# A gated linear recurrence followed by a two-layer MLP: 16-token rows of v read from the input, weight pieces laid out one by one, new due times

## The chip, the cores and the metric

The kernel runs on one core of a Trainium2 chip. The metric is device time in microseconds of one execution. The three runs of the kernel before took 986.98, 987.89 and 995.43 us; their median is 987.89 us.

## The reference

```python
mag = np.sqrt(a_re * a_re + a_im * a_im)
scale = np.minimum(mag, 0.999) / (mag + 1e-06)
a_re_n, a_im_n = (a_re * scale, a_im * scale)
...
for t in range(S):
    new_re = ar * S_re - ai * S_im
    new_im = ar * S_im + ai * S_re
    kv = np.einsum('bhd,bhe->bhde', k[:, :, t], v[:, :, t])
    S_re, S_im = (new_re + kv, new_im)
    y[:, :, t] = np.einsum('bhd,bhde->bhe', q[:, :, t], S_re)
...
x = np.ascontiguousarray(attn_out.transpose(0, 2, 1, 3)).reshape(B * S, H * D)
h = x @ w_in
g = np.maximum(h, 0.0) + alpha * np.minimum(h, 0.0)
return (g @ w_out).astype(np.float32)
```

There are 4 batches, 8 heads, 768 tokens and a head dimension of 48. x has 3072 rows of 384, w_in is 384 x 2048 and w_out 2048 x 384. The two weight matrices arrive as 64-bit floats; everything else is float32.

## The kernel before

**Units.** The 3072 tokens are cut into 24 units of 128 (4 batches x 6 chunks). A unit computes attention inside its chunk by levels: for h = 1, 2, 4, 8, 16, 32 the second half of each block of 2h tokens looks at the first half, and a state `St` carries what lies before the chunk. Six generators make one pipeline, and each engine executes in order what they gave it:

- `gates(b, c0, c1)`, nine in all: it normalizes the gates of one to three chunks, makes products of magnitudes (`decays_sb`, written to DRAM as `decs`) and running products of phases (written to DRAM as `phs`). Most of it is on ScalarE and VectorE; the products over short rows (L358, L360 with `blk`, `run`) are on GpSimd in all but the first gate.
- `loads()` (L614 to L632) brings q and k of a unit into `KQ` (three buffers), `phs` into `PP` (one buffer) and `decs` into `T` (two buffers).
- `half_rows()` (L598) copies v in DRAM into `vsc`, with only the first halves of blocks of h tokens, for each h in `SPREAD`; `loads_v()` (L641 to L664) brings v into `V`, and into `VL` the first halves for each level: for h = 1, 2, 32 straight from v (L661), for the h in `SPREAD` from `vsc` (L664). `V` and `VL` have two buffers.
- `pieces()` (L510) and `weights(name)` (L523 to L551) bring the weights in 8 pieces each of w_in and w_out, and turn 64-bit floats into float32: VectorE works on the bits (L528 to L541), PE adds high and low parts (L548, L549), ScalarE stores (L551).
- `unit(u)` (L681 to L850): the rotation of q and k by `PP` on VectorE (L681), the levels (PE L731 and L691; VectorE L735 to L750 and L711; ScalarE L708 and L756), keys transposed (L771, L775), the state (L783 to L799), the outputs `ps_y` (L823, L830), copied by ScalarE (L845) and written to DRAM as `ysc` (L850).
- `loads_x()` (L863) reads `ysc` back as `xT` for a group of units: groups of 1, 1, ten of 2, 1 and 1 units. `all_mlp()` gives each group 16 blocks of features (PE L874, ScalarE L882, VectorE L884), and the output matmuls L894, ScalarE L902, and L905 to DRAM.

**Order.** Nothing orders the work but the class `Plan`: every generator yields, ahead of each instruction, which engine it is for, what it costs and what it needs. The planner takes, of the steps that could start soonest, the one with the earliest due time. The due times are the numbers in `GATES_DUE`, `UNIT_DUE`, `UNIT_STEPS` and the two ends given to `plan.add`. All DMAs are issued by SyncE (SP), one after the other, in the planner's order; a DMA that has to wait for a buffer or for data holds up all that stand behind it.

Of the kernel before, what the change touches and what calls it, by code (L numbers as in the profile page):

```python
# [8 lines left out]
F32 = mybir.dt.float32  # L9
U32 = mybir.dt.uint32  # L10
AF = mybir.ActivationFunctionType
# [4 lines left out]
P = 128  # L16
# [115 lines left out]
def kernel(  # L132
# [32 lines left out]
    nc = tc.nc  # L165
    B, HP, _, D, S = q.shape
# [3 lines left out]
    NK = DM // P  # L170
# [54 lines left out]
    def DVE(n, *after, takes=(), first=False):  # L225
        return "DVE", 0.17 + n * 1.05e-3, after, takes, 0, first

    def ACT(n, *after, takes=(), first=False):
        return "ACT", 0.17 + n * 0.85e-3, after, takes, 0, first
# [29 lines left out]
    def gates(b, c0, c1):  # L259
# [66 lines left out]
        STT(out=dec[:, :, 0:P], in0=c.rearrange("p (m s) -> p m s", s=P), scalar=-2.0 * MAG_CAP,  # L326
            in1=f.rearrange("p (m s) -> p m s", s=P), op0=ALU.max, op1=ALU.mult)

        for o, (p, w) in enumerate(((y, -1.0), (x, 1.0), (y, 1.0))):
            tu = yield ACT(2.3 * N, tx, t)  # L330
            nc.scalar.activation(U3[:, o], p.rearrange("p (n l) -> p l n", l=L), AF.Copy, scale=w)  # L331
        at = 0
        while at < TL - 4:
            m = (TL - at) // 2
# [116 lines left out]
        done["gates", b + last, 0 if last else c1] = used  # L451


    w_in_sb = consts.tile([P, NK, DF], F32, tag="w_in_sb")
    w_out_sb = consts.tile([P, NF, DM], F32, tag="w_out_sb")


# [55 lines left out]
    def to_f32(dst, parts, scales, *key):  # L513

        n = 2 * DM
        ta = yield ACT(n, ("raw", *key), takes=(R["top"],))
        raw = raws.pop(key)
        lo, hi = raw[:, :, :, 0], raw[:, :, :, 1]
        rest = lo.bitcast(F32)
        slot = R["top"].taken  # L520
        top = tops[slot].rearrange("p (r e) -> p r e", r=dst.shape[1])
        top_u, dst_u = top.bitcast(U32), dst.bitcast(U32)
        nc.scalar.activation(top, hi.bitcast(F32), AF.Abs)  # L523
        tl = yield ACT(n, ta)
        nc.scalar.activation(rest, lo, AF.Copy, scale=2.0 ** -52)

        yield DVE(n // 2, ta)
        nc.vector.tensor_scalar(out=top, in0=top, scalar1=F64_SMALL, scalar2=None, op0=ALU.max)  # L528

        yield DVE(n * 3 // 4)  # L530
        nc.vector.tensor_scalar(out=dst_u, in0=top_u, scalar1=3, scalar2=0x3FFFFFFF,
                                op0=ALU.logical_shift_left, op1=ALU.bitwise_and)
        yield DVE(n)
        nc.vector.scalar_tensor_tensor(out=dst_u, in0=hi, scalar=0xC0000000, in1=dst_u,  # L534
                                       op0=ALU.bitwise_and, op1=ALU.bitwise_or)

        yield DVE(n * 3 // 4)
        nc.vector.tensor_scalar(out=top_u, in0=dst_u, scalar1=0xFF800000, scalar2=None,
                                op0=ALU.bitwise_and)
        t = yield DVE(n, tl)  # L540
        nc.vector.tensor_tensor(out=rest, in0=rest, in1=top, op=ALU.mult)  # L541
        R["top"].put(t, slot)
        for i, r in enumerate(parts):
            m, low = dst[:, r], rest[:, r]
            k = m.free_size()
            e = yield PE(k * 3.36e-3, t, takes=(R["h"],), n=2)
            p = ps.tile([P, 512], F32, tag="h", name="ps_w", bufs=2)[:, 0:k].rearrange("p (r e) -> p r e", r=m.shape[1])
            nc.tensor.matmul(p, lhsT=ident, rhs=m, start=True, stop=False)  # L548
            nc.tensor.matmul(p, lhsT=ident, rhs=low, start=False, stop=True)  # L549
            t_ = yield ACT(k, e)  # L550
            nc.scalar.activation(m, p, AF.Copy, scale=scales[i])  # L551
            R["h"].put(t_)
        raw_done(*key, e)
        return t_
# [11 lines left out]
    def weights(name):  # L566
        for f in range(NF // 2):
            if name == "in":
                dst, parts, scales = w_in_sb[:, :, 2 * f * P:2 * (f + 1) * P], (slice(0, 2), slice(2, 3)), (1.0, 1.0)
            else:  # L570
                dst, parts = w_out_sb[:, 2 * f:2 * (f + 1)], (slice(0, 1), slice(1, 2))
                scales = al_s[:, 2 * f:2 * f + 1], al_s[:, 2 * f + 1:2 * f + 2]
            done["w_" + name, 2 * f] = done["w_" + name, 2 * f + 1] = yield from piece(dst, parts, scales, name, f)


    KINDS = ["odd"] + LEVELS
    SPREAD = [4, 8, 16]
    vsc_of = {}

    def half_rows():  # L580
# [54 lines left out]
    def loads_v():  # L635
        for u in range(NU):
            b, c = divmod(u, NCH)
            yield DMA(196, ("KQ", u), takes=(R["V"],))
            L = loaded[u]
            L["V"] = V = work.tile([P, HP, D2], F32, tag="V", name="V", bufs=2)  # L640
            nc.sync.dma_start(V, v[b, :, :, c].rearrange("n p e -> p n e"))  # L641
            yield DMA(98)
            VL = work.tile([P, len(KINDS), 2, D2], F32, tag="VL", name="VL", bufs=2)
            first = True
            for k, h in enumerate(KINDS):
                for i in range(2):
                    tokens = v[b, 2 * i:2 * i + 2, :, c].rearrange("n t e -> t n e")
                    to = VL[HC * i:HC * (i + 1), k]
                    if h in ("odd", 1):
                        runs = [(to, tokens[int(h == "odd")::2])]  # L650
                    elif h == 2:
                        runs = [(to[j::2], tokens[j::4]) for j in range(2)]
                    elif h == 32:
                        runs = [(to[h * m:h * (m + 1)], tokens[2 * h * m:2 * h * m + h]) for m in range(2)]
                    else:
                        runs = []
                    for dst, src in runs:
                        if not first:
                            yield DMA(98 // len(runs))
                        first = False  # L660
                        nc.sync.dma_start(dst, src)  # L661
            t = yield DMA(98 * len(SPREAD), ("halves", u))
            k = KINDS.index(SPREAD[0])
            nc.sync.dma_start(VL[:, k:k + len(SPREAD)].rearrange("p l n e -> p l (n e)"),  # L664
                              vsc_of.pop(u).rearrange("l i t e -> (i t) l e"))
            L["Vp"] = {name: VL[:, i] for i, name in enumerate(KINDS)}
            done["V", u] = t
# [198 lines left out]
    def features(m, f):  # L866

        n = sizes[m] * P
        for kk in range(NK):
            e = yield PE(n * 1.68e-3, ("x", m), ("w_in", f), takes=() if kk else (R["h"],))  # L870
            if kk == 0:
                p = ps.tile([P, MT], F32, tag="h", name="ps_h", bufs=2)[:, 0:n]
            plan.pace = 1.0
            nc.tensor.matmul(p, lhsT=w_in_sb[:, kk, f * P:(f + 1) * P], rhs=x_of[m][:, kk],  # L874
                             start=(kk == 0), stop=(kk == NK - 1))
        if f == NF - 1:
            R["xT"].put(e)
# [51 lines left out]
    for name in ("own", 2, 4, 8):  # L929
# [2 lines left out]
    done["gates", 0, 0] = (0.0, None)  # L932

    GATES_DUE = [
        (145.8, -0.9), (-125.3, -261.5), (-2.2, 59.6), (112.1, 219.3), (145.0, -26.1),
        (358.3, 421.5), (448.3, 502.5), (551.6, 713.7), (655.6, 761.2)]
    UNIT_DUE = [
        (35.8, 100.2), (67.9, 143.4), (63.6, 187.3), (117.0, 222.5), (185.9, 230.8), (213.5, 204.9),
        (104.8, 306.5), (252.9, 331.0), (335.8, 397.3), (317.8, 425.7), (487.6, 432.7), (508.4, 489.4),
        (468.7, 487.1), (526.5, 660.8), (546.8, 535.6), (569.7, 615.2), (647.6, 662.7), (653.6, 773.1),  # L940
        (638.8, 733.1), (691.1, 812.1), (696.9, 905.6), (862.1, 912.0), (898.3, 879.4), (828.1, 948.6)]
    UNIT_STEPS = [
        0.40, 0.29, 0.46, -0.02, -0.03, 0.15, 0.15, 0.02, -0.25, -0.10, 0.03, -0.32,
        -0.33, 0.18, 0.04, 0.48, -0.09, -0.24, 0.58, 0.48, -0.53, -0.48, -0.50, -0.75,
        0.04, 0.14, -0.05, 0.53, 0.29, 0.37, -0.02, 0.39, 0.48, 0.01, 0.39, 0.82,
        1.53, 1.27, 0.88, 0.67, 1.33, 1.42, 0.91, 0.83, 0.36, 0.80, 0.71, 0.07,
        -0.52, 0.16, 0.60, -0.41, 0.38, 1.04, 0.53, 0.82, 0.72, 0.58]
    with tc.manual_schedule():
        for g, due in zip(GATES, GATES_DUE):
            plan.add(gates(*g), *due, 100)  # L950
        plan.add(loads(), -4.0, 841.6, 8 * NU)
        plan.add(half_rows(), 68.8, 993.5, 4 * (B + 1) * len(SPREAD))
        plan.add(loads_v(), 3.7, 887.5, 14 * NU)
        plan.add(pieces(), 17.0, 3.0, 33)
        plan.add(weights("in"), 5.3, 103.4, 11 * 8)
        plan.add(weights("out"), 12.4, 114.8, 11 * 8)
        for u in range(NU):
            plan.add(unit(u), *UNIT_DUE[u], 56, UNIT_STEPS)
        plan.add(loads_x(), -1.0, -1.0, 1)
        plan.add(all_mlp(), 925.1, 925.1, 1)  # L960
        plan.run()
# [37 lines left out]
```

## Time and profile before

| | |
|---|---|
| runs | 986.98, 987.89, 995.43 us |
| profiled execution | 986.92 us, its span 985.2 us |
| mean granted TensorE clock | 0.932 |
| DMA | 132.44 MB, mean 134 GB/s |
| first MLP matmul (L874) | 163.4 us |
| ps_y of the last unit (L823) | 879.0 us |

The span runs from the first to the last instruction. A row of a group of instructions names the line, the engine, the operation, out<-in with sizes and the count, then the busy time, the mean duration of one in ns, and the idle time ahead of it with what ended it. In a row by stretch each engine's busy time stands with its count of instructions. The chain of waits gives start, duration and what. SPq is SyncE's queue.

Steps of the kernel before, as the trace has them (us): the rotations (L681) of units 0 to 5 start at 46.3, 113.4, 153.1, 190.0, 219.6 and 242.6, their ps_y (L823) at 125.9, 190.1, 215.8, 249.3, 275.4 and 308.6. The last weight piece is stored at 190.2 us.

### The profile page before, as it was taken

How to read it: one execution, taken by the hardware profiler on the slowest of the kernel's cores; microseconds unless marked ns; L12 is line 12 of the kernel's file. 1: busy time of each engine (PE TensorE's matmuls, PEld its weight loads, DVE VectorE, ACT ScalarE, POOL GpSimd, SP SyncE). 2: the span in 40 equal slices, each digit the busy share in tenths (PEclk: the TensorE clock that was granted, in tenths of full speed). 3: DMA queues.
4: the chain of work that ended last, by engine and by line, in shares of the span. 5: the costliest groups of instructions: out<-in, count | busy, mean ns of one | idle time of the engine just before them, and what ended most of it. 6: DMA issues, size and time to landing. Idle time of an engine off the chain costs nothing.

```text
span 985.2 us, 24075 instructions
## 1 busy us (share of the span) xinstructions
PE 857.7 (87%) x9984; PEld 630.2 (64%) x9984; DVE 720.0 (73%) x1137; ACT 504.4 (51%) x942; POOL 163.8 (17%) x326
## 2 busy tenths in 40 slices
PE   0645647998699699999999998999999999999998
PEld 0312334776577577777677676777777767777776
DVE  6899898899779767889688776886687867621112
ACT  5566764784457346745754564545663533332122
POOL 3025026004300510043006000070004100000000
PEclk9867768999689599999999998999999999999999
DMA  6874993656576457573981667534934287400000
GB/s 191 209 200 133 224 241 85 167 137 149 132 206 158 103 153 175 134 191 103 225 215 27 172 165 152 147 86 137 199 108 102 69 161 136 100 18 25 17 9 17
DMA packets 190685, 132.44 MB, mean 134 GB/s; under 512 B 67568, under 2 KB 182384, under 8 KB 190576
## 3 DMA queue, kind: packets, MB, share of 16 engines
q1 hardware_dynamic: 190576, 130.90, 54.4%
q8 instruction: 79, 1.29, 0.6%
q14 instruction: 30, 0.25, 0.1%
HBM read 102.54 MB, written 35.68 MB: 140 GB/s over the span
## 4 chain that ended last, share of the span: by engine, by line
PE 69%; DVE 12%; POOL 6%; ACT 5%; issue 3%; DMA 3%; SPq 2%; DVEq 0%; ACTq 0%; POOLq 0%
PE ps_h L874 24%; PE ps_o L894 24%; PE ps_lv L691 7%; PE ps_y L823 4%; PE ps_kv L783 3%; PE ps_lv L731 2%; POOL blk L360 2%; POOL tmp L358 2%; PE ps_y L830 2%; DMA PP<-phs 2%; DVE tmp L358 2%; PE ps_kt L771 1%; DVE tmp L439 1%; DVE ab L323 1%; DVE tmp L360 1%
## 5 line engine op out<-in xcount | busy, mean ns | idle before, releaser
L874 PE MATMUL ps_h<-xT,w_in_sb 128*128 128x256 f32 (+1 forms) x1344 | 307.7, 360 | 2.9 <-DMA xT<-ysc 1.8
L894 PE MATMUL ps_o<-w_out_sb,g_sb 128*128 128x384 f32 x768 | 297.7, 503 | 1.1 <-DVE g_sb L884 1.1
L874 PEld LDWEIGHTS ps_h<-xT,w_in_sb 128*128 128x128 f32 x1344 | 232.7, 193 | 75.0 <-DVE g_sb L884 2.0
L882 ACT ACTIVATE g_sb<-ps_h,al 128x256 f32<-128x256 f32 (+1 forms) x224 | 99.2, 443 | 262.8 <-PE ps_h L874 261.4
L884 DVE SCALAR_TENSOR_TENSOR g_sb<-ps_h,al_sm,g_sb 128x256 f32<-128x256 f32 (+1 forms) x224 | 99.3, 443 | 156.5 <-ACT g_sb L882 155.3
L750 DVE TENSOR_TENSOR KQ<-KQ,T 96x512 f32<-96x512 f32 x240 | 168.1, 708 | 51.6 <-PE ps_lv L691 34.9
L894 PEld LDWEIGHTS ps_o<-w_out_sb,g_sb 128*128 128x128 f32 x768 | 136.2, 192 | 55.1 <-DVE g_sb L884 2.4
L691 PE MATMUL ps_lv<-KQ,W 96*64 96x64 f32 x1920 | 85.0, 235 | 27.6 <-ACT W L756 20.5
L691 PEld LDWEIGHTS ps_lv<-KQ,W 96*64 96x64 f32 x1920 | 70.2, 145 | 57.1 <-ACT W L756 28.4
L338 POOL TENSOR_TENSOR decays_sb<-decays_sb 128x72 f32<-128x72 f32 (+5 forms) x24 | 12.5, 520 | 466.1 <-DVE decays_sb L338 414.4
L756 ACT COPY W<-KQ 96x512 f32<-96x512 f32 x120 | 74.1, 624 | 7.7 <-DVE KQ L750 6.3
L681 DVE TENSOR_TENSOR KQ<-KQ,PP 96x2048 f32<-96x2048 f32 x24 | 55.2, 2301 | 9.4 <-DMA PP<-phs 7.2
L331 ACT ACTIVATE tmp<-ab 128x1152 f32<-128x1152 f32 (+2 forms) x27 | 56.3, 2109 | 1.9 <-DVE decays_sb L326 1.9
L548 PE MATMUL ps_w<-w_in_sb,ident 128*128 128x512 f32 (+1 forms) x32 | 19.7, 708 | 38.5 <-DVE w_in_sb L534 35.6
L845 ACT COPY yT<-ps_y 48x256 f32<-48x256 f32 x96 | 32.0, 366 | 39.7 <-PE ps_y L830 33.4
L708 ACT ACTIVATE A<-ps_lv,rows 128x64 f32<-128x64 f32 x144 | 38.1, 331 | 22.3 <-PE ps_lv L691 21.6
L358 POOL TENSOR_TENSOR tmp<-blk 128x72 f32<-128x72 f32 (+1 forms) x56 | 30.0, 535 | 105.1 <-ACT blk L389 101.3
L549 PE MATMUL ps_w<-g_sb,ident 128*128 128x384 f32 (+2 forms) x64 | 35.7, 646 | 12.7 <-DVE run L400 7.1
L783 PEld LDWEIGHTS ps_kv<-V,KT 64*96 64x96 f32 x704 | 37.8, 175 | 13.3 <-ACT KT L775 6.2
L783 PE MATMUL ps_kv<-V,KT 64*96 64x48 f32 x704 | 40.9, 261 | 4.8 <-ACT KT L775 4.8
L823 PE MATMUL ps_y<-A,VL 64*48 64x64 f32 x2304 | 45.1, 226 | 0.0
L358 DVE TENSOR_TENSOR tmp<-tmp 128x576 f32<-128x576 f32 (+2 forms) x63 | 43.4, 689 | 1.5
(115 smaller groups left out, 1075.0 us busy)
## 6 DMA issues: line engine op xcount, KB each, us to landing
T<-decs SPq DMA_DIRECT2D x48, 384.0 KB
KQ<-in_q_dram SPq DMA_DIRECT2D x48, 192.0 KB
KQ<-in_k_dram SPq DMA_DIRECT2D x48, 192.0 KB
PP<-phs SPq DMA_DIRECT2D x48, 192.0 KB
decs<-decays_sb SPq DMA_DIRECT2D x7, 1152.0 KB
phs<-tmp SPq DMA_DIRECT2D x14, 576.0 KB
vsc<-in_v_dram SPq DMA_DIRECT2D x48, 144.0 KB
VL<-vsc SPq DMA_DIRECT2D x24, 288.0 KB
```

The lines of the kernel that those rows point to most:

```text
L331: nc.scalar.activation(U3[:, o], p.rearrange("p (n l) -> p l n", l=L), AF.Copy, scale=w)
L358: on(4 * k).tensor_tensor(out=m, in0=w[:, 1::-1].unsqueeze(2).to_broadcast([P, 2, 2, k]), in1=pairs_of(u), op=ALU.mult)
L681: nc.vector.tensor_tensor(out=KQ, in0=KQ, in1=PP.unsqueeze(1).to_broadcast([D2, 2, H, P]), op=ALU.mult)
L691: nc.tensor.matmul(t[64 * i:64 * i + 64, p], lhsT=weights(4 * i + p), rhs=moving(KQ[:, 0, 4 * i + p]), start=True, stop=True)
L750: nc.vector.tensor_tensor(out=x, in0=x, in1=decays(h)[:, i].unsqueeze(3).to_broadcast([D2, H, n, h]), op=ALU.mult)
L756: nc.scalar.copy(W.rearrange("p n t -> p (n t)").rearrange("p (m h) -> p m h", h=h), halves(KQ[:, 1].rearrange("p n t -> p (n t)"), h)[:, ...
L783: nc.tensor.matmul(kv[s][:, n], lhsT=KT[rows, n], rhs=V[rows, n // 2, (n % 2) * D:(n % 2 + 1) * D], start=True, stop=True)
L823: nc.tensor.matmul(o, lhsT=vp[64 * i:64 * i + 64, s, e_ * D:(e_ + 1) * D], rhs=a[:, HC * own:HC * (own + 1)], start=(name == "own" and not ...
L874: nc.tensor.matmul(p, lhsT=w_in_sb[:, kk, f * P:(f + 1) * P], rhs=x_of[m][:, kk], start=(kk == 0), stop=(kk == NK - 1))
L882: nc.scalar.activation(gt, p, AF.Relu, scale=al_1[:, f:f + 1])
L884: nc.vector.scalar_tensor_tensor(out=gt, in0=p, scalar=al_sm[:, f:f + 1], in1=gt, op0=ALU.mult, op1=ALU.add)
L894: nc.tensor.matmul(sums[0], lhsT=gt[:, c * P:(c + 1) * P], rhs=w_out_sb[:, f], start=(f == 0), stop=(f == NF - 1))
```

## The change

`SPREAD` loses the 16, so `half_rows` makes two kinds of rows instead of three, and `loads_v` reads the first halves of the four 32-token stretches of each 64 rows straight from v, as it does for h = 32. `w_in_sb` is laid out by pieces. In `gates`, the negated copy is made from the transposed one. Some costs given to the planner change, and all due times are new.

```diff
-        for o, (p, w) in enumerate(((y, -1.0), (x, 1.0), (y, 1.0))):
+        for o, p in ((2, y), (1, x)):
             tu = yield ACT(2.3 * N, tx, t)
-            nc.scalar.activation(U3[:, o], p.rearrange("p (n l) -> p l n", l=L), AF.Copy, scale=w)
+            nc.scalar.copy(U3[:, o], p.rearrange("p (n l) -> p l n", l=L))
+        tu = yield ACT(N)
+        nc.scalar.activation(U3[:, 0], U3[:, 2], AF.Copy, scale=-1.0)
...
-    w_in_sb = consts.tile([P, NK, DF], F32, tag="w_in_sb")
+    w_in_sb = consts.tile([P, NF // 2, NK, 2 * P], F32, tag="w_in_sb")
...
-        yield DVE(n * 3 // 4)
+        yield DVE(n // 2)
         nc.vector.tensor_scalar(out=dst_u, in0=top_u, scalar1=3, scalar2=0x3FFFFFFF,
...
-                dst, parts, scales = w_in_sb[:, :, 2 * f * P:2 * (f + 1) * P], (slice(0, 2), slice(2, 3)), (1.0, 1.0)
+                dst, parts, scales = w_in_sb[:, f], (slice(0, 2), slice(2, 3)), (1.0, 1.0)
...
-    SPREAD = [4, 8, 16]
+    SPREAD = [4, 8]
...
-                    elif h == 32:
-                        runs = [(to[h * m:h * (m + 1)], tokens[2 * h * m:2 * h * m + h]) for m in range(2)]
+                    elif h >= 16:
+                        runs = [(to[h * m:h * (m + 1)], tokens[2 * h * m:2 * h * m + h]) for m in range(HC // h)]
...
-            nc.tensor.matmul(p, lhsT=w_in_sb[:, kk, f * P:(f + 1) * P], rhs=x_of[m][:, kk],
+            nc.tensor.matmul(p, lhsT=w_in_sb[:, f // 2, kk, f % 2 * P:(f % 2 + 1) * P], rhs=x_of[m][:, kk],
...
-        (145.8, -0.9), (-125.3, -261.5), (-2.2, 59.6), (112.1, 219.3), (145.0, -26.1),
-        (358.3, 421.5), (448.3, 502.5), (551.6, 713.7), (655.6, 761.2)]
+        (-251.5, -234.4), (-137.4, -381.1), (-121.1, -13.5), (186.7, 183.0), (96.1, 124.0),
+        (497.4, 308.3), (486.6, 518.2), (594.7, 624.3), (594.1, 831.0)]
...
-        plan.add(loads(), -4.0, 841.6, 8 * NU)
-        plan.add(half_rows(), 68.8, 993.5, 4 * (B + 1) * len(SPREAD))
-        plan.add(loads_v(), 3.7, 887.5, 14 * NU)
-        plan.add(pieces(), 17.0, 3.0, 33)
-        plan.add(weights("in"), 5.3, 103.4, 11 * 8)
-        plan.add(weights("out"), 12.4, 114.8, 11 * 8)
+        plan.add(loads(), 54.1, 931.2, 8 * NU)
+        plan.add(half_rows(), 16.8, 1036.5, 4 * (B + 1) * len(SPREAD))
+        plan.add(loads_v(), 236.4, 1199.2, 22 * NU)
+        plan.add(pieces(), -52.1, -100.2, 33)
+        plan.add(weights("in"), -26.9, 98.5, 11 * 8)
+        plan.add(weights("out"), -28.0, 124.3, 11 * 8)
```

`UNIT_DUE` and `UNIT_STEPS` are new as well; they are lists of the same kind and length, and are left out.

## The prediction

> **What bounds the kernel now.** I read first the busy times by engine, then the span in 40 slices, then stretches of it, and last the chain of waits inside the stretches that lose time.
>
> ```profile
> span 985.2 us, 24075 instructions
> PE 857.7 (87%) x9984; PEld 630.2 (64%) x9984; DVE 720.0 (73%) x1137; ACT 504.4 (51%) x942; POOL 163.8 (17%) x326
> ...
> PE   0645647998699699999999998999999999999998
> ...
> PEclk9867768999689599999999998999999999999999
> ```
>
> TensorE is the bound: it is idle for 985.2 - 857.7 = 127.5 us, and the digits put nearly all of that in the first seven slices and in slices 11 and 14, where the granted clock falls too. The same by stretch (busy time of PE, PEld, DVE, ACT, POOL with counts, then clock, DMA share, GB/s):
>
> ```profile
> 0.00:163.00 163.00, 78.88 (x568) 43.05 (x569) 140.61 (x237) 97.19 (x151) 46.14 (x95) 0.77 0.76 194
> 163.00:250.00 87.00, 79.09 (x1059) 62.51 (x1062) 78.97 (x129) 56.39 (x109) 19.82 (x34) 0.97 0.53 129
> 250.00:345.00 95.00, 77.69 (x1088) 62.19 (x1080) 77.74 (x114) 51.44 (x94) 19.27 (x40) 0.79 0.62 155
> 345.00:700.00 355.00, 341.24 (x4458) 254.67 (x4458) 274.17 (x408) 194.39 (x362) 62.69 (x122) 0.98 0.62 150
> ```
>
> Up to 163 us, where the first MLP matmul (L874) starts, PE idles 84 us and VectorE is the full engine (140.6 of 163). From 250 to 345 us PE idles 17 us and runs at 0.79 of its clock. After that little is left. The chain of waits names the two causes that I use (start, us, what):
>
> ```profile
> 99.29 2.27 SPq L598
> 101.60 2.86 SPq L598
> ...
> 261.15 1.70 SPq L661
> 266.95 4.50 DMA xT<-ysc
> ```
>
> At 98.6 to 106.6 us six copies of v (L598) stand ahead of PP of unit 1 in SP's queue, 1.33 us each; at 261 us SP is still issuing VL loads, and the xT that the MLP needs lands only at 271.5.
>
> [...]around both holes of the third stretch the clock is lowered (mean 0.79), so a gap costs more than its idle time. [...]The w_in piece is written today as 3 x 256[...], the w_out piece flat. The groups by shape agree:
>
> ```profile
> L531 DVE TENSOR_SCALAR w_in_sb<-top 128x768 uint32<-128x768 uint32 x8 | 7.6, 947 | 0.2
> L531 DVE TENSOR_SCALAR w_out_sb<-top 128x768 uint32<-128x768 uint32 x8 | 4.8, 600 | 0.1
> L331 ACT ACTIVATE tmp<-ab 128x1152 f32<-128x1152 f32 x21 | 49.2, 2356 | 1.9 <-DVE decays_sb L326 1.9
> ```
>
> **The change, part by part.** (1) *w_in piece by piece.* L531 and L538 on w_in become flat: 8 x (947 - 600) + 8 x (951 - 581) ns = 5.7 us less VectorE work, all before 167 us, where VectorE is the full engine. (2) *Gates.* One of three transposing copies (2.36 us at 1152 elements) becomes a flat negation; the flat ScalarE rows of that size are 1.16 us (L289), so 7 x 1.2 + 0.75 + 0.4 = 9.5 us less on ScalarE and 1.2 us less on each gate's chain. After the opening both lie under PE. (3) *v.* Blocks of 16 tokens come straight from v: 8 more issues per unit, 192 in all at 0.63 us (mean of L661), and 20 fewer vsc copies at 0.92 us (mean of L598): SP's issuing grows by 121 - 18 = 103 us on some 465 us. Nothing computes with SP, so this costs only where a PP, T or xT stands behind it. In bytes it saves a DRAM copy: 20 x about 0.12 MB written, and read again.
>
> (4) *Due times.* These reorder every queue. I took the built order of both programs and added up, per engine, what stands ahead of a step, at the trace's mean durations of the same line and shape (a matmul counts as its two passes). Before to after:
> - VectorE ahead of unit 0's rotation (L681): 36.6 to 27.2 us; of unit 1's: 97.7 to 94.3.
> - VectorE until unit 1's last L750: 160.5 to 137.2; unit 3's: 219.9 to 196.5; unit 5's: 265.6 to 251.7. Later units: within 12 us either way.
> - Last weight piece on VectorE (L541): 167.0 to 155.0.
> - PE ahead of the first L874: 73.6 to 82.6.
> - MLP feature blocks ahead of unit 3's ps_y: 32 to 19.
>
> *Opening.* Unit 0's rotation comes earlier in VectorE's queue than its PP can land, so I expect VectorE to wait some 4 us there; behind it stands the next gate's L293, which even so starts no later than before, with 9.4 us less ahead of it. SP then has four vsc copies instead of six ahead of PP of unit 1: 2 x 1.33 = 2.7 us earlier; the gate before it gains about 3 us in VectorE order, so rotation 1 starts near 108 us instead of 113.4. The first L874 now stands behind unit 2's first level, which needs VectorE at 145 us of its queue plus about 15 us of idle (15.7 before at rotation 1): about 160 us against 163.4, and PE has 9.0 us more behind it then. 9.0 + 3.4 = 12; I take **-11** (the unfinished overlap is unseen: 0 to -15).
>
> *The hole at 250 to 271 us.* By the same sums PE's time minus its work ahead grew from 94.2 us at unit 3's ps_y (249.3 - 155.1) to 107.8 at unit 4's: 13.6 us. Cause: unit 3's output is made just when the 32 feature blocks of units 0 and 1 are used up, so xT of units 2 and 3 is 8.2 us of PE work ahead of its use. After, 13 blocks are left, 23.7 us. From the end of ps_y to the issue of xT SP took 14.5 us in before for 14 issues (9.6 for 8, 17.3 for 14, 14.3 for 17: about 1.05 us each), and it took about 4 us more to the first use. After: 15 x 1.05 + 4 = 19.8 us, under 23.7. I take **-10** (-14 to +3).
>
> *The hole at 326 to 336 us.* It cost 13 us (107.0 to 120.2 between units 5 and 6): ScalarE stood in its queue waiting for GpSimd's chain of products (L387 for L360), with unit 6's copies behind it, and xT of units 4 and 5 was late. In after, xT stands 12.7 us of PE work ahead (13.3 before), 15 issues: still short by about 7. The wait for GpSimd has the same place in ScalarE's order. **-3** (-10 to +5).
>
> *Later groups.* xT of groups 5 to 9 loses slack: 43.8, 55.9, 41.8, 54.5, 53.4 us of PE work become 30.4, 22.3, 23.3, 25.7, 30.9, with 13 to 20 issues between, i.e. 17 to 25 us needed. Just hidden; **+3** (0 to +12). Unit loads of VL have two buffers and a unit's spacing of over 20 us, against 21 issues of 0.63 = 13 us: hidden; without that cover V would hold up L783.
>
> Sum: -11 - 10 - 3 + 3 = -21 us on the span of 985.2, i.e. 964. The profiled execution took 986.9 in all (1.7 around its span); the median of the runs, 987.9, is 1.0 above it. 964 + 2.7 = **967 us**.
>
> **The rivals.** *A, slower: SP becomes the wait.* xT stands behind up to 20 issues. For: in the opening SP needed 1.33 us for a vsc copy[...], and single issues took over 2 us. Against: away from there VL issues average 0.63 us. At 1.6 us per issue plus 4 us, xT is late by 4 us for group 0, 4 for group 2, 15, 12, 4, 10, 3 and 5 for groups 3 to 7 and 9: some 58 us with no gaps of before left (27) and the opening's 11 gained: 985 - 38 + 58 = 1005, and 1008 with the 2.7. It decides from about 1.4 us per issue, where the lateness equals the 38 gained. *B, no change: the gaps only move.* Three in-order queues wait for each other and for GpSimd (ScalarE for L360: 23.2 us in 8 waits); a new order makes new waits as long as those removed[...]. For: the same planner with the same costs ordered before, and left two such gaps. Against: unit 1 and 3 come 23 us of VectorE work earlier, far more than one such gap. Time: 985.2 - 4 (what of the 5.7 us of VectorE work lies on the path) + 2.7 = 984. *C, parts do not act:* the flat write keeps 947 ns. Then the opening loses up to 5.7 us of its 11: 972.
>
> **How the numbers follow.** Forecast (with C, 0.08, in it) 0.70; B 0.18; A 0.12. The forecast's bounds, -11 (0 to -15), -10, -3, +3, make 952 to 980, since not all ends meet. B adds up to about 988; what lies above is mostly A. Range 952 to 988. A measurement tells about 1% here (the three runs span 986.98 to 995.43), so faster means under 978, slower over 998: 0.70, 0.18 and 0.12.
>
> **What would show it.** Right: L531 on w_in_sb near 600 ns; the first L874 at or before 161 us; unit 3's ps_y before 232 us (249.3 now); no gap over 4 us with a releaser xT<-ysc between 240 and 290 us; PE idle near 105 us and fewer low PEclk digits in slices 11 and 14. Wrong: PE waits for xT<-ysc at several later groups with L661 ahead of L863 on SP (A), or as much PE idle as now with ScalarE or VectorE as releaser (B).

## The result, and the profile after

The kernel after takes **1020.27 us** (median of four runs, 1018.67 to 1024.2). The kernel before, run beside it, takes 990.07 us (four runs, 986.98 to 995.43). The ratio is 1.0305, with a 95% interval of 1.0247 to 1.0363: slower by 3%, where 967 us was forecast, and outside the range. The profiled execution took 1019.57 us, its span 1017.9 us.

In the code after, a line stands two further down than in the code before: v's direct loads are L663 (L661 before), the copies into `vsc` L600, the loads of q and k L616 and L618, PP L627, T L634, V L643, the loads from `vsc` L666, the rotation L683, ps_y L825, ysc L852, xT L865, and the MLP L876 and L896.

From the page of the kernel after: the busy times, PE and its clock in 40 slices, and the chain of waits by engine.

```profile
span 1017.9 us, 24317 instructions
PE 875.8 (86%) x9984; PEld 638.6 (63%) x9984; DVE 711.2 (70%) x1137; ACT 494.7 (49%) x942; POOL 159.5 (16%) x326
...
PE   0456746889997899998987999989998989999998
...
PEclk9877867898999899999998899999999998999999
...
PE 56%; DVE 11%; DMA 11%; SPq 8%; POOL 5%; ACT 5%; issue 3%; DVEq 0%; ACTq 0%; POOLq 0%
```

VectorE and ScalarE have less to do, by 8.8 and 9.7 us (5.7 and 9.5 were forecast). The span is 32.7 us longer in two parts of nearly one size: PE idles 14.6 us more (142.1 against 127.5), and is busy 18.1 us more with the same 9984 matmuls. The mean granted clock of the whole span is the same (0.933, before 0.932); from 345 to 930 us it is 0.97 instead of 0.99, so a lowered clock can explain a part of the 18.1 us (six L876 matmuls took 2.93 us from 334.88 us on, where the granted clock was 0.52, and 1.46 us from 338.40, where it was 1.00), and what the rest is stays open. Slice 11 no longer dips, slices 13 and 14 do, and so do later ones (19, 21, 22, 27, 31 and 33). The chain of waits of the kernel before was:

```profile
PE 69%; DVE 12%; POOL 6%; ACT 5%; issue 3%; DMA 3%; SPq 2%; DVEq 0%; ACTq 0%; POOLq 0%
```

So on the chain PE fell from 69% to 56%, while DMA rose from 3% to 11% and SyncE's queue from 2% to 8%. The same by stretch, with the columns as before:

```profile
0.00:163.00 163.00, 81.23 (x586) 45.05 (x587) 134.08 (x237) 95.79 (x155) 47.32 (x94) 0.79 0.74 188
163.00:250.00 87.00, 75.28 (x1070) 57.81 (x1069) 71.93 (x113) 48.89 (x90) 4.54 (x8) 0.88 0.60 142
250.00:345.00 95.00, 81.42 (x949) 62.54 (x948) 74.79 (x116) 51.66 (x94) 22.25 (x46) 0.93 0.56 139
345.00:700.00 355.00, 333.35 (x4241) 249.32 (x4243) 272.47 (x407) 183.41 (x352) 66.63 (x143) 0.97 0.59 136
700.00:900.00 200.00, 190.79 (x2413) 140.10 (x2404) 133.10 (x210) 85.46 (x178) 18.80 (x37) 0.97 0.54 117
```

The last stretch of the kernel before, for comparison:

```profile
700.00:900.00 200.00, 199.02 (x2430) 147.78 (x2430) 131.99 (x212) 85.58 (x180) 15.89 (x37) 1.00 0.46 102
```

From 345 to 700 us PE did 4241 matmuls; before it did 4458 (as the trace counts them: it has two records for each matmul of the program, 1344 at L876 for 672). In 700 to 900 us it idles 9.2 us, before 1.0. These counts cover different work, though, so I use another measure, worked out from the traces: **lateness**, a moment's time minus the work that PE has done by then, with each instruction counted at the median step of its line and shape over the runs. It grows where PE idles or runs slowly. In us, for the two kernels and the experiments that follow:

| kernel | at 163 | at 250 | at 345 | at 930 | from 345 to 930 |
|---|---|---|---|---|---|
| before | 87.5 | 97.3 | 129.9 | 172.1 | 42.2 |
| after | 87.5 | 108.2 | 130.8 | 203.8 | **73.0** |
| after, 16-token rows by way of vsc | 86.6 | 108.8 | 128.7 | 179.9 | 51.2 |
| that, with 192 tiny DMAs | 91.0 | 110.8 | 135.9 | 204.5 | 68.6 |
| before, new layout and gates | 87.5 | 97.4 | 129.5 | 170.3 | 40.8 |
| that, more rows by vsc from the second batch on | 86.3 | 96.9 | 128.5 | 161.6 | 33.1 |

The kernel after is level with before at 163 us and at 345 us. It loses nearly all of its 31 us after 345 us, in the stretch that I had called nearly free. There is no single hole in it. Compared with the same order with the 16-token rows by way of `vsc`, the units' ps_y run level up to unit 5, and then fall behind by about 1.3 us per unit, to 24 us at unit 23.

SyncE shows what is new. Its queue's timeline at one place (start, us, issues):

```profile
437.80 0.45 SPq L616 DMA_DIRECT2D KQ<-in_q_dram  x1
...
440.88 12.17 SPq L663 DMA_DIRECT2D VL<-in_v_dram  x20
453.10 1.13 SPq L666 DMA_DIRECT2D VL<-vsc  x1
454.27 0.70 SPq L600 DMA_DIRECT2D vsc<-in_v_dram  x1
455.08 0.94 SPq L634 DMA_DIRECT2D T<-decs  x2
...
456.63 0.38 SPq L616 DMA_DIRECT2D KQ<-in_q_dram  x1
```

The waits of SyncE in the same kernel (who waited for what: us, times, longest):

```profile
SPq L616 <- PE ps_y L832: 54.5, 14, 8.5
SPq L634 <- DVE St L798: 48.8, 10, 20.9
SPq L852 <- ACT yT L847: 41.2, 11, 19.3
```

The first of these was 10.4 us before. (With the same order and the 16-token rows by way of `vsc`, a run below, it is 55.7 us: this wait belongs to the new order, not to the added loads.) So SyncE stands still until PE gives back a `KQ` buffer, and then has a burst to issue: q, k, PP, V, and then 20 loads of VL, which alone take 12.2 us. What comes behind them, T, and q and k of the next unit, starts that much later. A piece of the chain of waits of the kernel after runs through such a burst (start, us, what):

```profile
365.30 5.48 DMA KQ<-in_k_dram
370.80 0.60 SPq L663
...
375.30 1.39 SPq L663
...
383.81 4.95 DMA phs<-tmp
...
393.89 9.87 DMA KQ<-in_q_dram
```

SyncE's issues in all, in the traces: 736, which take 464 us, before; 908, which take 525 us, after. The theories start here. **V:** v's 192 direct loads make the loss; its rival is that the new order of all queues (the due times) makes it, and v's loads are innocent. If V holds, the question is how they do it: by the time that SyncE takes to **issue** them, with whatever stands behind (**I**), or by their transfers, bytes and small packets (**L**). Issues that carry next to no bytes tell the issuing time from the bytes. **D** stands in the expectations for the rival of V, the due times.

### The profile page after: what moved, and what is told of

Same layout as the page of the kernel before. It is cut to its first block, busy times and chain, and to the rows that moved or that the text cites. A ratio compares the mean times of both kernels' runs of the same rounds, so it can differ in the third digit from the quotient of the medians.

```text
span 1017.9 us, 24317 instructions
## 1 busy us (share of the span) xinstructions
PE 875.8 (86%) x9984; PEld 638.6 (63%) x9984; DVE 711.2 (70%) x1137; ACT 494.7 (49%) x942; POOL 159.5 (16%) x326
## 4 chain that ended last, share of the span: by engine, by line
PE 56%; DVE 11%; DMA 11%; SPq 8%; POOL 5%; ACT 5%; issue 3%; DVEq 0%; ACTq 0%; POOLq 0%
PE ps_o L896 21%; PE ps_h L876 19%; PE ps_lv L693 5%; SPq L663 5%; PE ps_y L825 4%; PE ps_kv L785 2%; POOL tmp L360 2%; POOL blk L362 2%; PE ps_y L832 2%; DVE tmp L360 2%; DVE tmp L441 2%; DMA VL<-in_v_dram 1%; DMA T<-decs 1%; PE ps_lv L733 1%; DMA KQ<-in_k_dram 1%
## 5 line engine op out<-in xcount | busy, mean ns | idle before, releaser
L876 PE MATMUL ps_h<-xT,w_in_sb 128*128 128x256 f32 (+1 forms) x1344 | 307.9, 362 | 11.0 <-DMA xT<-ysc 11.0
L896 PE MATMUL ps_o<-w_out_sb,g_sb 128*128 128x384 f32 x768 | 305.2, 512 | 9.3 <-issue 6.1
L876 PEld LDWEIGHTS ps_h<-xT,w_in_sb 128*128 128x128 f32 x1344 | 236.0, 196 | 83.7 <-DMA xT<-ysc 12.2
L896 PEld LDWEIGHTS ps_o<-w_out_sb,g_sb 128*128 128x128 f32 x768 | 135.0, 193 | 64.4 <-issue 9.5
L693 PEld LDWEIGHTS ps_lv<-KQ,W 96*64 96x64 f32 x1920 | 71.2, 147 | 67.6 <-ACT W L758 32.7
L340 POOL TENSOR_TENSOR decays_sb<-decays_sb 128x72 f32<-128x72 f32 (+5 forms) x24 | 9.4, 394 | 450.2 <-DVE decays_sb L340 448.9
L683 DVE TENSOR_TENSOR KQ<-KQ,PP 96x2048 f32<-96x2048 f32 x24 | 55.0, 2293 | 14.1 <-issue 6.8
L360 POOL TENSOR_TENSOR tmp<-blk 128x72 f32<-128x72 f32 (+1 forms) x56 | 35.0, 625 | 135.4 <-ACT blk L391 90.0
L825 PE MATMUL ps_y<-A,VL 64*48 64x64 f32 x2304 | 49.0, 220 | 0.0
L825 PEld LDWEIGHTS ps_y<-A,VL 64*48 64x48 f32 x2304 | 44.3, 122 | 1.6 <-issue 1.2
L441 DVE TENSOR_TENSOR tmp<-tmp,off 128x2304 f32<-128x2304 f32 (+2 forms) x18 | 41.1, 2284 | 1.8 <-ACT off L434 1.6
```

The source lines that it names most:

```text
L360: on(4 * k).tensor_tensor(out=m, in0=w[:, 1::-1].unsqueeze(2).to_broadcast([P, 2, 2, k]), in1=pairs_of(u), op=ALU.mult)
L441: TT(out=m, in0=UT, in1=turned(off3, o).unsqueeze(2).to_broadcast([P, 2, L, nb]), op=ALU.mult)
L683: nc.vector.tensor_tensor(out=KQ, in0=KQ, in1=PP.unsqueeze(1).to_broadcast([D2, 2, H, P]), op=ALU.mult)
L693: nc.tensor.matmul(t[64 * i:64 * i + 64, p], lhsT=weights(4 * i + p), rhs=moving(KQ[:, 0, 4 * i + p]), start=True, stop=True)
L825: nc.tensor.matmul(o, lhsT=vp[64 * i:64 * i + 64, s, e_ * D:(e_ + 1) * D], rhs=a[:, HC * own:HC * (own + 1)], start=(name == "own" and not ...
L876: nc.tensor.matmul(p, lhsT=w_in_sb[:, f // 2, kk, f % 2 * P:(f % 2 + 1) * P], rhs=x_of[m][:, kk], start=(kk == 0), stop=(kk == NK - 1))
```

## The experiments

All kernels compute the reference's output in full; those with tiny DMAs add work and leave none out. "Issues" are SyncE's as the traces have them; the expectations count two more in each kernel. Where an edit says that the planner is given the old steps, the order of the other four engines is the same as in the kernel that the edit starts from. Each was measured against the kernel before in runs beside it: its medians were 985.07, 986.96, 984.36 and 982.3 us in the four sets below.

### First set: each part by itself

**After, with the 16-token rows by way of `vsc` again** (736 issues; the planner is given the steps of after):

```diff
-    SPREAD = [4, 8]
+    SPREAD = [4, 8, 16]
+    PLANNED = [4, 8]
...
+                        if h != 16:
+                            nc.sync.dma_start(dst, src)
```

> The changed kernel with its v part undone and nothing else: the 16-token rows go through vsc again (3 kinds of rows, 738 SP issues instead of 910), while every instruction of the other engines keeps its place, because the planner is given the same steps. Theory V (the 192 added issues hold up q, k, PP, T and xT in SP's queue): most of the 30 us comes back, 985 to 1000 us. Theory D (the new due times make a worse order, whatever SP does): 1010 to 1022 us. In between, 1000 to 1010, both have a share.

Measured: 994.75 us, ratio 1.0118 (1.0065 to 1.0171), against 1.0305 (1.0247 to 1.0363) for after, and within the 985 to 1000 us of theory V. Undoing the v part alone takes back 18 us by the ratios, 25 us by the medians; the profiled spans differ by 24.5 us (993.4). On its chain of waits SyncE's queue is back at 2% and DMA at 6%:

```profile
span 993.4 us, 24081 instructions
...
PE 65%; DVE 10%; POOL 7%; ACT 7%; DMA 6%; issue 3%; SPq 2%; DVEq 0%; ACTq 0%; POOLq 0%
```

**Before, with the v part alone** (908 issues; order of before):

```diff
-    SPREAD = [4, 8, 16]
+    SPREAD = [4, 8]
+    PLANNED = [4, 8, 16]
...
+                    if h == 16:
+                        for m in range(4):
+                            nc.sync.dma_start(to[h * m:h * (m + 1)], tokens[2 * h * m:2 * h * m + h])
```

> The kernel before with the v part alone: 16-token rows straight from v (192 issues more, 20 vsc copies fewer), every other engine's order as before. Theory V: 1005 to 1020 us. Theory D: 985 to 997 us, since before has slack of 40 to 56 us of PE work ahead of the later groups.

Measured: 993.67 us, ratio 1.0101 (1.003 to 1.0171): slower by about 10 us. That is in the range of theory D (985 to 997 us) and a miss for V, which wanted 1005 us or more. By the middle values the same edit costs about half as much in the order of before as in that of after, but the intervals overlap. That its price depends on what stands behind the loads in the queue is suggested by this, not shown.

**Before, with the w_in layout and the gates' copy alone:**

```diff
-    w_in_sb = consts.tile([P, NK, DF], F32, tag="w_in_sb")
+    w_in_sb = consts.tile([P, NF // 2, NK, 2 * P], F32, tag="w_in_sb")
...
+                nc.scalar.activation(U3[:, 0], U3[:, 2], AF.Copy, scale=-1.0)
```

> The kernel before with the flat w_in pieces and the flat negated copy of the gates alone, every engine's order as before. Both theories: 982 to 990 us, since 5.7 us of VectorE and 9.5 us of ScalarE go, and only what lies before 163 us is on the path. If it is over 995, the layout itself has a cost that neither theory has.

Measured: 983.93 us, ratio 0.9993 (0.996 to 1.0026): nothing. In its trace the rotations of units 0, 1 and 2 start at 45.9, 113.4 and 152.3 us, before at 46.3, 113.4 and 153.1. The saved 5.7 us of VectorE and 9.5 us of ScalarE were not on the path at any of these points.

**After, planned with the due times of before** (every other part of the change kept):

```diff
-        plan.add(loads(), 54.1, 931.2, 8 * NU)
-        plan.add(half_rows(), 16.8, 1036.5, 4 * (B + 1) * len(SPREAD))
+        plan.add(loads(), -4.0, 841.6, 8 * NU)
+        plan.add(half_rows(), 68.8, 993.5, 4 * (B + 1) * len(SPREAD))
...
```

> The changed kernel with all due times of before (loads_v keeps its 22 steps per unit), so v, layout and gates as changed, ordered by the old numbers. Theory V: 1010 to 1025 us. Theory D: 982 to 998 us.

Measured: 1046.13 us, ratio 1.0642 (1.0575 to 1.071), a miss for both theories. Since the planner sees other steps and costs, old numbers make a third order, not the old one. Such a swap doesn't price the due times.

### Second set: issues or bytes, and whose queue

**Rows by way of `vsc`, and 192 tiny DMAs at the places of the direct loads.** It starts from the first experiment's kernel. Each tiny DMA brings 16 x 2 x 16 numbers into a part of VL that nothing reads, 0.39 MB in all, while the real ones bring 12 KB each. The number of packets is not less, though: 48 for each DMA, tiny or real (the tiny ones raise the queue's count from 190576 to 199792).

```diff
+                        else:
+                            nc.sync.dma_start(VL[HC * i + h * m:HC * i + h * (m + 1), len(KINDS), :, 0:16], src[:, :, 0:16])
```

> The changed kernel with its 16-token rows through vsc (994.75 us) plus, at the places of the direct loads, 192 DMAs of 16 x 2 x 16 numbers into a part of VL that nobody reads: the issues without the bytes, every other engine's order unchanged. If SP's issuing time is the cost (theory I): 1012 to 1024 us. If it is the transfers or where the data land (theory L): 993 to 1000 us.

Measured: 1022.02 us, ratio 1.0367 (1.0289 to 1.0445). That is in the range of theory I, and the whole loss is back, 27 us above the same kernel without them by the medians (25 by the ratios), although no result depends on them. SyncE's queue at one unit of the kernel with tiny DMAs (L671 are the tiny ones, L669 real loads):

```profile
448.87 5.39 SPq L669 DMA_DIRECT2D VL<-in_v_dram  x8
454.30 4.47 SPq L671 DMA_DIRECT2D VL<-in_v_dram  x8
458.81 1.83 SPq L669 DMA_DIRECT2D VL<-in_v_dram  x4
...
463.47 2.00 SPq L639 DMA_DIRECT2D T<-decs  x2
```

Eight DMAs of 2 KB take 4.47 us to issue, 0.56 each; eight real loads, of 24 and 48 KB, take 5.39 us, 0.67 each, and the four of 24 KB that follow 0.46 each. The queue pays here by the DMA, hardly by its bytes. **So the loss of the v part comes with the issues, without their bytes.** The small packets are not excluded by this run, since it keeps their number; but the 16 DMA engines are busy only some 8 us longer with them (54.6% of 1018.0 us against 55.1% of 993.4), while SyncE issues for 562 us instead of 476.

**After, with GpSimd issuing the 16-token loads:**

```diff
-                        nc.sync.dma_start(dst, src)
+                        (nc.gpsimd if h == 16 else nc.sync).dma_start(dst, src)
```

> The changed kernel with the eight 16-token loads per unit issued by GpSimd instead of SP, in the same places of the planner's order; same bytes. Theory I: SP is relieved of 192 issues, so 990 to 1005 us, unless GpSimd, waiting for VL's buffer, holds up the gates' products, which would bring it over 1020. Theory L: 1015 to 1025 us.

Measured: 1006.11 us, ratio 1.0196 (1.0135 to 1.0257). That misses the 990 to 1005 us of theory I by 1 us, and is far from the 1015 us at which L begins. By the medians 14 of the 25 us are back, by the ratios 11 of 18, with the same bytes; only 3072 of the small packets are gone. So by the middle values SyncE's issuing makes the larger part of the loss, though the intervals of the two ratios just overlap; why the rest does not come back is open. On the chain SyncE's queue is at 1% and DMA at 3%, but GpSimd's busy time grew from 159.5 to 253.3 us, and it waits 197.8 us for PE to give back a `VL` buffer, with its products for the gates behind these loads. SyncE's issuing falls from 525 to 431 us: about half a microsecond per DMA is small, but one queue pays it 908 times.

**Before, planned with the due times of after:**

```diff
-        plan.add(loads(), -4.0, 841.6, 8 * NU)
+        plan.add(loads(), 54.1, 931.2, 8 * NU)
...
```

> The kernel before, unchanged but for the due times, which are those of the changed kernel. With v and layout as before and the new order. If the new due times are worse by themselves: over 1000 us. If they fit any version: 985 to 998 us, as the changed order with vsc gave 994.75.

Measured: 1052.14 us, ratio 1.066 (1.0573 to 1.0747). By what was expected, over 1000 us means that the new due times are worse by themselves. But the other swap went the same way, and the new order with the rows by way of `vsc` took only 994.75 us. I take it that either set of numbers fits only the version that it was chosen for; the two swaps don't show more.

**Before with the new layout, and the rows of 2 and 32 tokens by way of `vsc` too** (584 issues):

```diff
-    SPREAD = [4, 8, 16]
+    SPREAD = [2, 4, 8, 16, 32]
+    PLANNED = [4, 8, 16]
+    ALSO = {4: [(1, 4), (0, 2)], 8: [(2, 8)], 16: [(3, 16), (4, 32)]}
```

> The kernel before with the flat w_in pieces and the gates' copy (983.9 us), and the other way round in v: also the rows of 2- and 32-token blocks go through vsc, so 8 direct loads per unit fewer and 40 copies more, 586 issues by SP; every other engine's order as before. Theory I: 975 to 984 us (the direct loads cost 9 us in this order, so fewer should bring something). Theory L, or copies in DRAM that are late at the start: 984 to 1000 us.

Measured: 992.22 us, ratio 1.0061 (1.0038 to 1.0084). Fewer issues, and still slower: a miss for theory I, which wanted 975 to 984 us. SyncE's queue of this kernel shows a place where it loses:

```profile
101.94 0.65 SPq L282 DMA_DIRECT2D ab<-in_a_im_dram  x1
102.64 18.95 SPq L607 DMA_DIRECT2D vsc<-in_v_dram  x12
121.64 1.12 SPq L634 DMA_DIRECT2D PP<-phs  x2
```

Twelve copies stand ahead of unit 1's PP where six stood, and rotation 1 starts at 126.7 us, 13 us late. The copies for the first batch cost time in the opening, where DMA is busiest (in the kernel before a share of 0.76 up to 163 us, then 0.53 to 0.62 up to 700 us); those for the later batches were still untried.

### Third set: fewer issues, where they cost nothing

**The same, but only from the second batch on** (616 issues):

```diff
+    EARLY = [4, 8, 16]
+    LATE = [2, 4, 8, 16, 32]
```

> The order of before with flat w_in pieces and gates' copy; the first batch as in before, from the second batch on also the 2- and 32-token rows through vsc: 618 issues by SP instead of 738, and no added copy ahead of unit 1's PP. In the run with vsc from the start PE was 13 us late at unit 1 and only 3 to 4 us late at the end, so theory I says 972 to 980 us. If that late gain was chance: 982 to 990 us.

Measured: **975.73 us** (973.43 to 980.34), ratio 0.9918 (0.9893 to 0.9943): faster than before by 0.8% (0.6 to 1.1), and in the range of theory I. Its page:

```profile
span 974.9 us, 23924 instructions
PE 856.7 (88%) x9984; PEld 629.4 (65%) x9984; DVE 714.0 (73%) x1137; ACT 493.8 (51%) x942; POOL 165.3 (17%) x326
```

PE idles 118.2 us (127.5 before), and the lateness from 345 to 930 us falls to 33.1 us. This suggests that SyncE's issuing cost the kernel before some microseconds as well, in a stretch where PE was 96% busy (341.24 of 355 us from 345 to 700 us). It is not shown by itself: SyncE's issuing falls only from 464 to 449 us, and the way in which v's rows reach the chip changes too.

**All seven kinds by way of `vsc` from the second batch on** (568 issues):

```diff
-    LATE = [2, 4, 8, 16, 32]
+    LATE = ["odd", 1, 2, 4, 8, 16, 32]
```

> The same, with all seven kinds of rows through vsc from the second batch on, one VL load per unit: 570 issues, but each row crosses DRAM twice more. Theory I: 968 to 980 us. If the bytes of the copies become the limit: over 985 us.

Measured: 988.6 us, ratio 1.0045 (1.0021 to 1.007), a miss: 13 us slower than with five kinds, with fewer issues. It moves 139.49 MB, with five kinds 135.96. The likely cause is those bytes; no run takes them apart from the further copies that each batch then needs.

**The order of after, with the same cut** (616 issues, edit as above):

> The changed kernel's order on all other engines, with v as in the first of these: 16-token rows through vsc always, 2- and 32-token rows too from the second batch on; 618 issues instead of 910. If the rest of the changed kernel's loss (994.75 us with 738 issues) is SP as well: 975 to 986 us. If it is the order itself: 990 to 997 us.

Measured: 999.0 us (992.41 to 1003.4), ratio 1.0138 (1.007 to 1.0207), no better than with 736 issues (1.0118), and nearest to the 990 to 997 us that were expected if the order itself is to blame. What after's order still loses, about 12 us by the ratios 1.0118 and 0.9993, was not mended by fewer issues.

**After, with GpSimd issuing the 14 loads of xT:**

```diff
-            nc.sync.dma_start(x_of[m], ysc_of.pop(m).rearrange("(k p) s -> p k s", p=P))
+            nc.gpsimd.dma_start(x_of[m], ysc_of.pop(m).rearrange("(k p) s -> p k s", p=P))
```

> The changed kernel with the 14 xT loads issued by GpSimd, so that they pass SP's queue of VL loads; all else as changed. If xT behind SP's issues is what costs (rival A in its own form): 1000 to 1010 us. If the lateness comes through q, k, PP, T and V as well: 1012 to 1020 us.

Measured: 1021.67 us, ratio 1.0374 (1.0313 to 1.0436): no gain, and just above both ranges. xT, which my sum and rival A watched, is not where the issues act: in the kernel after, PE waits for it 11.0 us in all, and only 1.9 us of that lie between 345 and 930 us. In this run it is still 7.3 us.

### Fourth set: which place in the queue

Both start from the first experiment's kernel, and add eight tiny DMAs per unit from unit 6 on, 144 in all, into a tile that nothing reads. They differ in the place: **ahead of the load of q**, or **behind the unit's loads of VL**.

```diff
+        for m in range(8):
+            nc.sync.dma_start(spare[16 * m:16 * (m + 1)], v[b, 0:2, 16 * m:16 * (m + 1), c, 0:16].rearrange("n t e -> t n e"))
...
+            if u >= NCH:
+                more(b, c)
```

> The changed order with 16-token rows through vsc (994.75 us), plus eight small DMAs per unit, from unit 6 on, into a tile that nobody reads, ahead of the unit's first q load. If only issues inside the burst count (theory P): SP waits some 55 us in all for the q buffers there and takes part of the 144 x 0.6 us in that time, 996 to 1008 us. If every issue counts wherever it stands (theory E): 1012 to 1024 us.

> The same eight small DMAs per unit, from unit 6 on, at the end of the unit's v loads, behind VL and ahead of what follows (T, PP, the next q). If the late VL is what costs, 995 to 1003 us; if what stands behind it costs (T, PP, phs), or if every issue counts, 1010 to 1024 us.

Measured: 1008.23 us, ratio 1.026 (1.0179 to 1.0342), ahead of q; 1018.03 us, ratio 1.0352 (1.029 to 1.0415), behind VL. Behind VL the loss is nearly that of all 192, though no VL load of the same unit stands behind the tiny DMAs. So the lateness of that VL isn't needed; what else stands behind in the queue is enough. Ahead of q the time lies just above what was expected if SyncE's wait for a buffer hides a part (996 to 1008 us). The trace fits: q's load waits 12.4 us there for its buffers, against 55.7 us without the tiny DMAs and 50.5 with them behind VL. But the two intervals overlap, and ahead of q the tiny DMAs themselves wait another 46.4 us, which the trace puts down to the landing of T; so the difference in place is only suggested.

## Why the prediction was wrong

It forecast 964 us for the span and got 1017.9. The lateness divides the miss: up to 345 us the sum said -24, and +1 came; after that it said +3, and +31 came. Of these 31, 22 go with the v part (73.0 to 51.2 in the table) and 9 are left in the new order without it (51.2 to 42.2).

**The step that failed most: "Later groups", +3 (0 to +12).** It came from xT's slack alone, with "Nothing computes with SP, so this costs only where a PP, T or xT stands behind it" and VL's 21 issues "hidden". The parts of it:
- *The issuing time was mis-sized, on the safe side.* I added 192 x 0.63 - 18 = 103 us; SyncE's total rose by 61: the loads of VL take 91 us more instead of 121 (one L663 takes 0.48 us at the median against 0.60 for L661 before), and the copies 28 us less instead of 18.
- *The cover was wrong.* I compared 13 us of VL issues with a unit's spacing of over 20, as if SyncE had the time between free. It does not: it waits 54.5 us for q's buffers, 48.8 for `St` and 41.2 for yT, and each wait is followed by a burst, so what stands behind the added issues comes later. The tiny DMAs show that the issues make the loss without their bytes, and those behind VL that a unit's own VL needn't be late.
- *The list was cut short.* I worked out slack for xT and for VL, and none for q, k, PP or T. Moving xT to another queue gained nothing. In the traces VectorE's waits for T (L737 in the kernel after) between 345 and 930 us are 4.3 us with the rows by way of `vsc`, 8.9 in the kernel after, and 10.5 and 12.3 with tiny DMAs at the places of the loads and behind VL; with them ahead of q the wait is for PP (12.5 us, 4.5 without them). That points to T and PP as two of the ways, but is too small to be all.

**"Opening", -11 (0 to -15): 0.** The sizes were right: L531's work on w_in takes 602 ns (forecast 600, an estimate from the flat w_out piece), and the gates' flat copy 1165 ns (1.16 us). By shape, in the kernel after:

```profile
L533 DVE TENSOR_SCALAR w_in_sb<-top 128x768 uint32<-128x768 uint32 x8 | 4.8, 602 | 0.2
...
L333 ACT ACTIVATE tmp<-tmp 128x1152 f32<-128x1152 f32 x7 | 8.2, 1165 | 0.0
```

They were worth nothing by themselves: VectorE is the busiest engine there (134.1 of 163 us), but with these parts alone in the order of before the steps start when they did. Rotation 1 came at 111.3 us instead of 108. Rotation 2 started at 158.2 us, 21 us after the 137.2 us of VectorE work that I had added up ahead of it, where I took 15 us of idle from before; and the first MLP matmul came at 173.1 us, not at 160. PE's timeline of the kernel after (start, us, line, idle time ahead and its releaser) shows what stood in front of it:

```profile
165.24 1.10 PE L550 MATMUL ps_w<-w_in_sb,ident 128*128 128x512 f32 x2 [1.32 <-DVE w_in_sb L536]
166.97 1.87 PE L551 MATMUL ps_w<-g_sb,ident 128*128 128x512 f32 x2 [0.64 <-DVE g_sb L543]
...
173.08 1.60 PE L876 MATMUL ps_h<-xT,w_in_sb 128*128 128x128 f32 x12
...
334.88 2.93 PE L876 MATMUL ps_h<-xT,w_in_sb 128*128 128x256 f32 x6 [9.04 <-DMA xT<-ysc]
```

Weight pieces, waiting for VectorE, still came just before it, and PE's first matmul of all was at 28.3 us instead of 17.9. The 9 us more of PE work ahead was used up by that: at 163 us the lateness is 87.5 in both kernels. From 163 to 250 us it then grows by 20.7 us, before by 9.8.

**"The hole at 250 to 271", -10: about right.** It closed; unit 3's ps_y came at 238.1 us (249.3 before; forecast before 232), and the lateness from 250 to 345 us grew by 22.6 instead of 32.6. But it only gave back what had been lost from 163 to 250 us. That loss belongs to the new order: with the rows by way of `vsc` the lateness at 250 us is the same (108.8). No run takes it apart further. **"The hole at 326 to 336", -3: about 0.** It is there again, 9.04 us in the last line above, on the same wait.

**The rivals.** A, "SP becomes the wait", had the right engine, and by luck nearly the right end (1008 of 1020), but the wrong price (from 1.4 us per issue; it was about 0.5) and the wrong place: PE waits for xT 11.0 us in all, of which 1.9 us lie in the stretch that loses, and a run without SyncE's xT issues gains nothing. B named ScalarE and VectorE; only some of its reasoning, a new order with new waits, fits the rest of the loss. C falls, since the parts took the times that were forecast.

**The account of the 3.05%:** the v part is 1.9% (1.0305 less 1.0118, each with an interval of some 0.5% to either side), shown for the order of after; the order and the due times 1.2% (1.0118 less 0.9993), by subtraction only; layout and gates nothing in the order of before (0.9993), shown. Still open: by which of q, k, PP, T and phs the lateness reaches PE, what share the small packets have in it, and what after's order loses apart from SyncE. More buffers for q and V weren't tried.

## What to carry to other kernels

Price a DMA by its place in the issuing queue, not by its bytes or by the queue's mean load (here 192 DMAs of 2 KB cost 27 us by the medians): list everything that stands behind it, and ask which of those loads is issued only after a buffer comes free. SyncE's queue worked in bursts here, with 54.5 us of waiting for q's buffers and 20 loads of VL issued in 12.2 us at one unit, so its idle share was no cover. Test such a queue with tiny DMAs that nothing reads; where they bring the loss, issue fewer or issue elsewhere (1006.11 us with GpSimd issuing, against 1020.27), and keep the copies that save issues out of the stretch in which the DMA engines are busiest (992.22 us with them in it, at a DMA share of 0.75 up to 163 us; 975.73 with them only from the second batch on).

## What was not expected of the hardware

- The time that SyncE took to issue a DMA hardly went with its size: 0.56 us for one of 2 KB, 0.46 to 0.67 us for real loads of VL, of 24 and 48 KB, in the same unit. Over the whole trace of the kernel with tiny DMAs the medians are 0.42 us for the 192 of 2 KB and 0.46 us for the 48 loads of T with 384 KB.
- An xT load takes GpSimd 0.83 us to issue, and SyncE 0.42 us in the kernel after (medians of 14). A 16-token load of VL takes GpSimd 0.50 us (median of 192).
- The same work in another order of its engines, with no part of it changed, moved the time by over 60 us: 1052.14 against 986.96.
